# Linear attention, soft mixture and ELU layer on one core: r scaled on its way out of PSUM, the bonus product read from PSUM, the weight conversion spread over two steps

## The chip, the cores and the metric

The kernel runs on one core of one Trainium2 chip. Its time is device microseconds (us) of one execution; the figure for the kernel before is the median of three runs.

## The reference

Three layers follow each other, all in float32. The attention has 4 sequences of 768 tokens and 8 heads of 48 columns; its output, 3072 tokens by 384 columns, goes through a soft mixture of 8 experts with 4 slots each, and then through a dense layer of width 2048.

```python
for t in range(S):                       # attention
    cur = einsum('bhd,bhe->bhde', u * k[t], v[t])
    y[t] = einsum('bhd,bhde->bhe', r[t], state + cur)
    state = w * state + einsum('bhd,bhe->bhde', k[t], v[t])
logits = x @ phi                         # soft mixture: 32 slots
slot_in = softmax(logits, over tokens).T @ x
slot_out[e] = relu(slot_in[e] @ w1[e]) @ w2[e]
z = softmax(logits, over slots) @ slot_out
h = z @ w_in                             # dense layer
out = where(h > 0, h, exp(min(h, 0)) - 1) @ w_out
```

`w_in` and `w_out` come as float64. The chip has no float64 arithmetic here, so the kernel reads each number as two 32-bit words and builds a float32 from them.

## The kernel before, in words

The order on every engine is written out by hand: an engine runs its instructions in the order in which the code issues them, and one that waits holds up all behind it on that engine.

**The attention** cuts the 3072 tokens into 24 chunks of 128 (`NCH`), six to a sequence. The loop `for s in range(-2, NCH)` is a software pipeline over three chunks. In step s it does:

- for chunk s+2: load r and k a step or two ahead, multiply them by tables of powers of w (`scale`, L515: r on GpSimd, k on VectorE, into `rkm`), and turn both by TensorE (`turn`: `ps_r`, `ps_k`), copied out of PSUM by ScalarE to `rT` and `kT`.
- for chunk s+1: add k'v to the state in PSUM (`update`, `pu`), carry the state over (`state`, `t1` on VectorE, `qc` on GpSimd, `qb` on ScalarE), the scores `ps_a` and their mask (`causal`, `am`), the elementwise product of rT and kT (`prod`, `qd`, VectorE) whose sums give the bonus term with u (`bonus_a`, `bonus_b`: `ps_b`, `bt`, `ps_c`, `bs`, and `bv` on GpSimd), and the part of the rows that comes from the earlier state (`before`, into `py`).
- for chunk s: the rest of its rows (`rows_a`, into `py`), their sum with the bonus (`rows_b`, `x`, VectorE), and their turn (`x_T`, `ps_x`).

Three chunks make a group, and a group's logits and slot sums (`part`: `slots_a` to `slots_f`) are dealt out over the following steps by `extra()`, one entry at a time.

**The conversion** of the first 10 of 16 tiles of `w_in` and `w_out` runs in the same loop, one piece of 384 columns a step in steps 0 to 19: `wide_load` brings the raw words into one of two buffers in `scr`, `wide_a` is two ScalarE instructions, `wide_b1`, `b2`, `b3` and `c` are four of VectorE, `wide_d` two of GpSimd. The expert weights (`load_we`) are fetched in the loop as well, on the same queue of SyncE (SP) as r, k, v and the raw words.

**The experts** follow: `up` and `down` of two halves of four experts (a = 0, 1), `turn(a)` between them, `turn_so(a)` behind `down(a)`; ScalarE meanwhile copies all turned weights of the second softmax (`turn_c_b`, `cT`) and splits the converted `w_out` in two (`split`). **The dense layer** is last; the change leaves it alone.

The pools of PSUM that matter are `pt_p`, two buffers that `ps_r`, `ps_x` and `ps_k` take in turn, and `pm_p`, two buffers for the bonus and the slots. `rkm` and `kT` have one buffer, `rT` two.

## Time and profile before

| | |
|---|---|
| median of three runs (lowest to highest) | 472.33 us (471.44 to 473.89) |
| the profiled execution, its own time | 471.74 us |
| its span, first to last instruction | 470.0 us |
| TensorE's clock, mean granted | 0.985 of 2.4 GHz |
| busy: TensorE, VectorE, ScalarE, GpSimd | 89%, 79%, 60%, 40% of the span |
| fetched from memory, written | 51.96 MB, 4.72 MB |

The profiled execution is one program run taken by the hardware profiler; its busy shares are means over three layers that have different limits, so a change to one layer is read in that layer's stretch. In the views, PE is TensorE, PEld its weight loads, DVE VectorE, ACT ScalarE, POOL GpSimd, SP SyncE. L515 is line 515 of the kernel before.

### The profile page before, as it was taken

How to read it: one execution, taken by the hardware profiler on the slowest of the kernel's cores; microseconds unless marked ns; L12 is line 12 of the kernel's file. 1: busy time of each engine (PE TensorE's matmuls, PEld its weight loads, DVE VectorE, ACT ScalarE, POOL GpSimd, SP SyncE). 2: the span in 40 equal slices, each digit the busy share in tenths (PEclk: the TensorE clock that was granted, in tenths of full speed). 3: DMA queues.
4: the chain of work that ended last, by engine and by line, in shares of the span. 5: the costliest groups of instructions: out<-in, count | busy, mean ns of one | idle time of the engine just before them, and what ended most of it. 6: DMA issues, size and time to landing. Idle time of an engine off the chain costs nothing.

```text
span 470.0 us, 10112 instructions
## 1 busy us (share of the span) xinstructions
PE 416.3 (89%) x4013; PEld 365.3 (78%) x4013; DVE 373.7 (79%) x550; ACT 281.4 (60%) x512; POOL 188.9 (40%) x186
## 2 busy tenths in 40 slices
PE   6788788797888898995999899989999999999995
PEld 6677677676776685343899789979998989999994
DVE  5489999979989854533787999996999987787851
ACT  3355455454564452293778787865879677776740
POOL 2276776666866731400000235431224314224440
PEclk9799999989999999999899999999999999999999
DMA  8848899998999987670000111121111001011112
GB/s 124 183 94 232 189 262 257 271 280 206 244 262 273 231 275 237 234 270 1 0 2 0 33 35 34 35 67 35 34 35 33 1 0 51 35 52 67 69 69 73
DMA packets 97575, 57.41 MB, mean 122 GB/s; under 512 B 77808, under 2 KB 89328, under 8 KB 97520
## 3 DMA queue, kind: packets, MB, share of 16 engines
q1 hardware_dynamic: 96704, 56.64, 44.0%
q8 instruction: 33, 0.54, 0.5%
q14 instruction: 22, 0.18, 0.1%
q10 hardware_dynamic: 816, 0.05, 0.1%
HBM read 51.96 MB, written 4.72 MB: 121 GB/s over the span
## 4 chain that ended last, share of the span: by engine, by line
PE 46%; DVE 9%; ACT 5%; issue 4%; POOL 0%; ACTq 0%; DVEq 0%
PE fo L1258 11%; PE fo L1261 11%; PE fo L1259 11%; PE fh L1213 3%; DVE ex L1227 3%; DVE ex L1232 3%; PE pd L1035 2%; PE ph L1013 2%; ACT th L1221 2%; ACT acc L1195 1%; PE phm L1131 1%; ACT gh L1240 1%; ACT ex L1224 1%; PE py L613 1%; DVE acc L1202 0%
## 5 line engine op out<-in xcount | busy, mean ns | idle before, releaser
L1258 PE MATMUL fo<-wh,gh 128*128 128x384 f32 x384 | 131.8, 343 | 7.0 <-ACT gh L1240 3.7
L1259 PE MATMUL fo<-wl,gh 128*128 128x384 f32 x384 | 130.3, 339 | 0.0
L1261 PE MATMUL fo<-wh,gl 128*128 128x384 f32 x384 | 121.9, 339 | 0.2 <-DVE gl L1243 0.2
L1258 PEld LDWEIGHTS fo<-wh,gh 128*128 128x128 f32 x384 | 72.5, 189 | 13.9 <-ACT acc L1195 6.5
L1227 DVE SCALAR_TENSOR_TENSOR ex<-ex,th 128x1024 f32<-128x1024 f32 (+1 forms) x52 | 62.1, 1194 | 23.3 <-ACT ex L1224 23.0
L336 POOL TENSOR_TENSOR cv<-raw,cv 128x384 f32<-128x384 f32 x12 | 19.8, 1652 | 138.2 <-DVE cv L333 65.9
L1221 ACT ACTIVATE th<-fh 128x1024 f32<-128x1024 f32 (+1 forms) x53 | 50.3, 949 | 41.1 <-PE fh L1213 41.1
L1243 DVE TENSOR_TENSOR gl<-ex,gh 128x1024 fp32r<-128x1024 f32 (+1 forms) x52 | 72.0, 1385 | 2.6 <-ACT gh L1240 2.2
L1259 PEld LDWEIGHTS fo<-wl,gh 128*128 128x128 f32 x384 | 72.6, 189 | 1.8
L1261 PEld LDWEIGHTS fo<-wh,gl 128*128 128x128 f32 x384 | 71.9, 189 | 0.5 <-DVE gl L1243 0.5
L1232 DVE SCALAR_TENSOR_TENSOR ex<-ex,fh 128x1024 f32<-128x1024 f32 (+1 forms) x52 | 58.7, 1130 | 0.1
L1224 ACT ACTIVATE ex<-fh 128x1024 f32<-128x1024 f32 (+1 forms) x53 | 50.3, 950 | 9.5 <-DVE gl L1243 9.4
L1240 ACT CAST gh<-ex 128x1024 fp32r<-128x1024 f32 (+1 forms) x52 | 51.5, 991 | 5.9 <-DVE ex L1232 4.7
L1200 POOL TENSOR_TENSOR acc<-os,acc 128x384 f32<-128x384 f32 x20 | 29.0, 1486 | 49.6 <-ACT os L1199 49.6
L602 POOL TENSOR_TENSOR bv<-vd,bs 128x384 f32<-128x384 f32 x24 | 28.3, 1180 | 13.6 <-ACT bs L597 11.5
L1213 PE MATMUL fh<-cT,mst 128*128 128x512 f32 x96 | 30.6, 400 | 2.8 <-DVE ex L1232 2.8
L560 DVE TENSOR_TENSOR am<-ps_a,mask 128x512 f32<-128x512 f32 x48 | 30.6, 675 | 1.5 <-PE ps_a L555 1.5
L529 ACT COPY rT<-ps_r 128x512 f32<-128x512 f32 x24 | 14.1, 587 | 28.5 <-PE ps_r L522 28.5
L533 DVE TENSOR_TENSOR qd<-rT,kT 128x512 f32<-128x512 f32 x24 | 28.9, 1202 | 2.0 <-ACT kT L526 2.0
L522 PE MATMUL ps_r<-ident,rkm 128*128 128x128 f32 x96 | 15.7, 286 | 16.6 <-POOL rkm L515 15.8
L522 PEld LDWEIGHTS ps_r<-ident,rkm 128*128 128x128 f32 x96 | 10.1, 140 | 25.2 <-POOL rkm L515 22.9
L555 PE MATMUL ps_a<-rT,kT 64*128 64x128 f32 x384 | 28.8, 291 | 0.2 <-ACT kT L526 0.2
(170 smaller groups left out, 737.4 us busy)
## 6 DMA issues: line engine op xcount, KB each, us to landing
we<-in_moe_w_dram SPq DMA_DIRECT2D x14, 768.0 KB, 7.8
we<-in_moe_w_dram SPq DMA_DIRECT2D x16, 512.0 KB, 5.8
rk<-in_r_dram SPq DMA_DIRECT2D x24, 192.0 KB, 5.4
rk<-in_k_dram SPq DMA_DIRECT2D x24, 192.0 KB, 4.8
vd<-in_v_dram SPq DMA_DIRECT2D x24, 192.0 KB, 5.3
out_dram<-acc SPq DMA_DIRECT2D x24, 192.0 KB, 1.9
we<-in_moe_w_dram SPq DMA_DIRECT2D x16, 256.0 KB, 5.2
scr<-in_moe_w_out_dram SPq DMA_DIRECT2D x10, 384.0 KB, 4.2
```

The lines of the kernel that those rows point to most:

```text
L560: nc.vector.tensor_tensor(out=am[n, a], in0=aps[a], in1=mask.unsqueeze(1).to_broadcast([128, HP, 128]), op=ALU.mult)
L1200: nc.gpsimd.tensor_tensor(out=a, in0=os_, in1=a, op=ALU.add)
L1213: nc.tensor.matmul(out=ph[n][:, i, :], lhsT=mst[(f + i) // 8][:, 128 * ((f + i) % 8):128 * ((f + i) % 8) + 128], rhs=cT[:, TB * blk:TB * b ...
L1221: nc.scalar.activation(out=th[n][:, s], in_=ph[n][:, s], func=ACTF.Tanh, scale=0.5)
L1224: nc.scalar.activation(out=ex[n][:, s], in_=ph[n][:, s], func=ACTF.Exp)
L1227: nc.vector.scalar_tensor_tensor(out=ex[n][:, s], in0=ex[n][:, s], scalar=1.0, in1=th[n][:, s], op0=ALU.add, op1=ALU.mult)
L1232: nc.vector.scalar_tensor_tensor(out=ex[n][:, s], in0=ex[n][:, s], scalar=0.0, in1=ph[n][:, s], op0=ALU.min, op1=ALU.max)
L1240: nc.scalar.copy(out=gh[n][:, s], in_=ex[n][:, s])
L1243: nc.vector.tensor_tensor(out=gl[n][:, s], in0=ex[n][:, s], in1=gh[n][:, s].bitcast(F32), op=ALU.subtract)
L1258: nc.tensor.matmul(out=o, lhsT=gh[n][:, i, s], rhs=wh, start=(f == first), stop=False)
L1259: nc.tensor.matmul(out=o, lhsT=gh[n][:, i, s], rhs=wl, start=False, stop=False)
L1261: nc.tensor.matmul(out=o, lhsT=gl[n][:, i, s], rhs=wh, start=False, stop=(f == final))
```

## The change

Five edits, all in the attention loop, its end, and the order of the experts.

1. r is no longer scaled before it is turned. It is loaded into `rp` (two buffers with zeroed gaps), turned raw, and VectorE multiplies it by the table `vt` as it leaves PSUM for `rT`. GpSimd's `scale` of r and ScalarE's copy of `ps_r` are gone; the table is no longer turned.
2. The bonus product `qd` reads k from PSUM (`ps_k`), right behind `kT`'s copy, and is issued in `turn(1, n)` at the end of the step before; `prod` is gone.
3. `wide_b1` moves from VectorE to GpSimd, `wide_a` from the end of a step to the start of the next, `wide_b3` and `wide_c` to the end of the step, and `wide_d` to the next step. The raw words have three buffers.
4. In the last step the three entries of the group before come first, with the logits of two of the last three chunks, so that only the third chunk's logits follow its turn.
5. Among the experts `turn(1)` comes before `down(0)`, `turn_so(0)` behind `down(1)`, and one split moves behind `down(0)`.

```diff
@@ -315,4 +315,4 @@
 
-    def wide_b1(raw, a):
-        nc.vector.tensor_scalar(
+    def wide_b1(raw, a, eng=None):
+        (eng or nc.vector).tensor_scalar(
             out=a.bitcast(F32), in0=a.bitcast(F32), scalar1=EXP_LO, scalar2=EXP_HI, op0=ALU.max, op1=ALU.min
@@ -411,5 +411,5 @@
         pw = at2.tile([128, 2, HP, 65], F32, tag="am", name="pw", bufs=3)
-        vt = at2.tile([128, HP, 128], F32, tag="am", name="vt", bufs=3)
+        vt = ae1.tile([128, HP, 128], F32, name="vt")
         vk = at2.tile([128, HP, 128], F32, tag="am", name="vk", bufs=3)
-        wrk = ae1.tile([128, 2, H, D], F32, name="wrk")
+        wk = ae1.tile([128, H, D], F32, name="wk")
         ri = at1.tile([128, HP, 17], F32, name="ri")
@@ -459,7 +459,6 @@
             nc.scalar.copy(out=vk[:, :, 64:128], in_=pw[:, 1, :, 1:65])
-            for i, t in ((0, vt), (1, vk)):
-                ps = pt_p.tile([128, 512], F32, tag="pt", name="ps_wk")
-                for p in range(HP):
-                    nc.tensor.transpose(out=ps[:, 128 * p:128 * p + 128], in_=t[:, p, 0:128], identity=ident)
-                nc.scalar.copy(out=wrk[:, i], in_=ps.rearrange("p (h d) -> p h d", d=64)[:, :, 0:D])
+            ps = pt_p.tile([128, 512], F32, tag="pt", name="ps_wk")
+            for p in range(HP):
+                nc.tensor.transpose(out=ps[:, 128 * p:128 * p + 128], in_=vk[:, p, 0:128], identity=ident)
+            nc.scalar.copy(out=wk, in_=ps.rearrange("p (h d) -> p h d", d=64)[:, :, 0:D])
 
@@ -492,3 +491,4 @@
 
-        rkm = ae1.tile([128, 2, H, 64], F32, name="rkm")
+        rp = [ae2.tile([128, H, 64], F32, name=f"rp{i}", bufs=1) for i in range(2)]
+        km = ae1.tile([128, H, 64], F32, name="km")
         kT = ae1.tile([128, HP, 128], F32, name="kT")
@@ -500,9 +500,11 @@
 
-        def load_rk(n, which=(0, 1)):
+
+        def load_r(n):
             b, c = divmod(n, NC)
-            s = slice(C * c, C * c + C)
-            for i in which:
-                a = (r, k)[i]
-                rk[i, n] = ae2.tile([128, H, D], F32, tag=f"rk{i}", name=f"rk{i}", bufs=2)
-                nc.sync.dma_start(out=rk[i, n], in_=a[b, :, s, :].rearrange("h p d -> p h d"))
+            nc.sync.dma_start(out=rp[n % 2][:, :, 0:D], in_=r[b, :, C * c:C * c + C, :].rearrange("h p d -> p h d"))
+
+        def load_k(n):
+            b, c = divmod(n, NC)
+            rk[n] = ae2.tile([128, H, D], F32, tag="rk1", name="rk1", bufs=2)
+            nc.sync.dma_start(out=rk[n], in_=k[b, :, C * c:C * c + C, :].rearrange("h p d -> p h d"))
 
@@ -513,6 +515,4 @@
 
-        def scale(i, n, eng=None):
-            (eng or (nc.gpsimd, nc.vector)[i]).tensor_tensor(
-                out=rkm[:, i, :, 0:D], in0=rk.pop((i, n)), in1=wrk[:, i], op=ALU.mult
-            )
+        def scale(n):
+            nc.vector.tensor_tensor(out=km[:, :, 0:D], in0=rk.pop(n), in1=wk, op=ALU.mult)
 
@@ -522,3 +522,4 @@
                 nc.tensor.transpose(
-                    out=ps[:, p, :], in_=rkm[:, i, 2 * p:2 * p + 2, :].rearrange("p a d -> p (a d)"), identity=ident
+                    out=ps[:, p, :], in_=(km if i else rp[n % 2])[:, 2 * p:2 * p + 2, :].rearrange("p a d -> p (a d)"),
+                    identity=ident,
                 )
@@ -526,9 +527,7 @@
                 nc.scalar.copy(out=kT, in_=ps)
+                qd[n] = at2.tile([128, HP, 128], F32, tag="qd", name="qd", bufs=1)
+                nc.vector.tensor_tensor(out=qd[n], in0=rT[n], in1=ps, op=ALU.mult)
             else:
                 rT[n] = at2.tile([128, HP, 128], F32, tag="rT", name="rT", bufs=2)
-                nc.scalar.copy(out=rT[n], in_=ps)
-
-        def prod(n):
-            qd[n] = at2.tile([128, HP, 128], F32, tag="qd", name="qd", bufs=1)
-            nc.vector.tensor_tensor(out=qd[n], in0=rT[n], in1=kT, op=ALU.mult)
+                nc.vector.tensor_tensor(out=rT[n], in0=ps, in1=vt, op=ALU.mult)
 
@@ -542,3 +541,3 @@
                     nc.tensor.matmul(
-                        out=pu[64 * a:64 * a + D, p, :], lhsT=rkm[:, 1, 2 * p + a, 0:D], rhs=vd[n][:, 2 * p + a, :],
+                        out=pu[64 * a:64 * a + D, p, :], lhsT=km[:, 2 * p + a, 0:D], rhs=vd[n][:, 2 * p + a, :],
                         start=True, stop=True,
@@ -785,3 +784,2 @@
         scr = we_p.tile([128, KD * FE], F32, tag="we", name="scr").bitcast(I32)
-        sca = ae1.tile([128, PW], I32, name="sca")
         wiv, wov = win.rearrange("p k f -> p (k f)"), wo.rearrange("p i f -> p (i f)")
@@ -801,4 +799,4 @@
             n = min(PW, NW - PW * j)
-            raw = scr[:, 2 * PW * (j % 2):2 * PW * (j % 2) + 2 * n].rearrange("p (n t) -> p n t", t=2)
-            return raw, (sca[:, :n] if j % 2 else scr[:, 4 * PW:4 * PW + n])
+            raw = scr[:, 2 * PW * (j % 3):2 * PW * (j % 3) + 2 * n].rearrange("p (n t) -> p n t", t=2)
+            return raw, scr[:, PW * (6 + j % 2):PW * (6 + j % 2) + n]
 
@@ -817,2 +815,5 @@
                 raw, a = piece(j)
+                if f is wide_b1:
+                    f(raw, a, nc.gpsimd)
+                    return
                 if f is not wide_d:
@@ -829,6 +830,8 @@
 
-        load_rk(0)
+        load_r(0)
+        load_k(0)
         load_v(0)
         nc.scalar.dma_start(out=phi_sb, in_=phi.rearrange("(k p) c -> p k c", p=128))
-        nc.gpsimd.memset(rkm[:, :, :, D:], 0.0)
+        for t in (*rp, km):
+            nc.gpsimd.memset(t[:, :, D:], 0.0)
         nc.gpsimd.memset(uw, 0.0)
@@ -841,5 +844,5 @@
         tables()
-        load_rk(1)
+        load_r(1)
+        load_k(1)
         load_v(1)
-        scale(0, 0, nc.vector)
         nwe = 0
@@ -854,3 +857,2 @@
         for s in range(-2, NCH):
-            j = s
             now, nxt, ahead = s >= 0, 0 <= s + 1 < NCH, s + 2 < NCH
@@ -859,10 +861,11 @@
                 update(s + 1)
-            if ahead and s > -2:
-                scale(0, s + 2)
-            if j == -1:
-                wide(0, wide_a)
-            if not last:
+            wide(s, wide_a)
+            wide(s, wide_b1)
+            if last:
+                extra()
+                extra()
+                extra()
+                logits(GS - 1, 0, G - 1)
+            else:
                 extra()
-            if ahead:
-                scale(1, s + 2)
             if s > 0 and s % G == 0:
@@ -873,13 +876,11 @@
                 state(s + 1)
-                prod(s + 1)
+            if ahead:
+                scale(s + 2)
             if 2 <= s + 4 < NCH:
-                load_rk(s + 4, (1,))
+                load_k(s + 4)
             if 2 <= s + 3 < NCH:
                 load_v(s + 3)
-            if 2 <= s + 4 < NCH:
-                load_rk(s + 4, (0,))
-            if s < 0:
+            if s < 1:
                 wide_load(s + 2)
             if now:
-                wide(j, wide_b1)
                 for p in range(HP):
@@ -887,2 +888,6 @@
                 rows_b(s)
+                wide(s, wide_b2)
+                wide(s - 1, wide_d)
+                if s >= 1 and s + 2 < NP:
+                    wide_load(s + 2)
             if nxt:
@@ -893,10 +898,3 @@
                 bonus_c(s + 1)
-            if now:
-                wide(j, wide_b2)
-                wide(j, wide_b3)
-                wide(j, wide_c)
-                wide(j, wide_d)
-            extra()
-            if last:
-                extra()
+            if not last:
                 extra()
@@ -904,2 +902,4 @@
                 turn(0, s + 2)
+            if 2 <= s + 4 < NCH:
+                load_r(s + 4)
             if nxt:
@@ -910,5 +910,7 @@
             if last:
-                logits(GS - 1)
+                logits(GS - 1, G - 1, G)
             if nxt:
                 bonus_b(s + 1)
+            wide(s, wide_b3)
+            wide(s, wide_c)
             if ahead:
@@ -917,6 +919,2 @@
                 state_b(s + 1)
-            if j >= 0:
-                wide(j + 1, wide_a)
-                if j + 2 < NP:
-                    wide_load(j + 2)
             if s == NCH - 2:
@@ -927,3 +925,3 @@
                 nwe += 1
-            if j == NP - 1:
+            if s == NP:
                 assert nwe == NWE - 1
@@ -1091,14 +1089,14 @@
     turn_c_b(0)
+    turn(1)
     turn_c_a(1)
     turn_c_a(2)
-    for i in range(0, 4):
+    for i in range(0, 3):
         split(i)
     down(0)
-    turn(1)
     turn_c_b(1)
-    turn_so(0)
     turn_c_b(2)
-    for i in range(4, FA // 2):
+    for i in range(3, FA // 2):
         split(i)
     down(1)
+    turn_so(0)
     turn_so(1)
```

**TensorE, one step in the middle of the loop** (the second half of step s, from the turn of r on; the names in brackets are the engines or queues whose signal the instruction waits for). Before:

```order
L522 MATMUL ps_r<-ident,rkm 128x128 [waits Pool_49]
L522 MATMUL ps_r<-ident,rkm 128x128 x3
L613 MATMUL py<-qb_145,rT 128x96 [waits DVE_49,Activation_49]
L613 MATMUL py<-qb_145,rT 128x96 x3
L645 MATMUL ps_x<-ident,x 128x128 x3
L595 MATMUL ps_c<-ident,bt 128x128 [waits Activation_49]
L522 MATMUL ps_k<-ident,rkm 128x128 [waits Activation_49]
```

And now:

```order
L522 MATMUL ps_r<-ident,rp_144 128x128 [waits DMAHW3_49]
L522 MATMUL ps_r<-ident,rp_144 128x128 x3
L612 MATMUL py<-qb_147,rT 128x96 [waits DVE_49,Activation_49]
L612 MATMUL py<-qb_147,rT 128x96 x3
L644 MATMUL ps_x<-ident,x 128x128 x3
L594 MATMUL ps_c<-ident,bt 128x128 [waits Activation_49]
L522 MATMUL ps_k<-ident,km 128x128 [waits DVE_49]
```

The order is the same. The turn of r waits for its transfer where it waited for GpSimd, and the turn of k waits for VectorE (which must have emptied r's buffer) where it waited for ScalarE.

**VectorE, one step in the middle of the loop**, from the carry of the state to the next one; `scr` is the raw words under conversion, `al` and `nmx` the maxima of a group's logits. Before:

```order
L583 TENSOR_TENSOR t_147<-qc,pu 128x192 [waits Pool_49]
L533 TENSOR_TENSOR qd<-rT,kT 128x512 [waits Activation_49]
L317 TENSOR_SCALAR scr<-scr 128x384 [waits Activation_49]
L636 TENSOR_TENSOR x<-py,bv 128x384 [waits PE_49,Pool_49]
L560 TENSOR_TENSOR am<-ps_a,mask 128x512 [waits PE_49] x2
L322 TENSOR_SCALAR scr<-scr 128x384 [waits DVE_49]
L328 SCALAR_TENSOR_TENSOR scr<-scr 128x384 [waits DMAHW3_49,DMAHW2_49,DVE_49]
L333 TENSOR_SCALAR scr<-scr 128x384 [waits DVE_49]
L670 TENSOR_REDUCE al<-ps_l 96x1 [waits PE_49]
L671 TENSOR_SCALAR nmx<-al,nmx 96x1 [waits DVE_49]
L515 TENSOR_TENSOR rkm<-rk_856,wrk 128x8x48 [waits DMAHW0_49,PE_49]
```

And now:

```order
L582 TENSOR_TENSOR t_149<-qc,pu 128x192 [waits PE_49,Pool_49]
L517 TENSOR_TENSOR km<-rk_726,wk 128x8x48 [waits DMAHW7_49]
L635 TENSOR_TENSOR x<-py,bv 128x384 [waits PE_49,Pool_49]
L322 TENSOR_SCALAR scr<-scr 128x384 [waits Pool_49]
L559 TENSOR_TENSOR am<-ps_a,mask 128x512 [waits PE_49] x2
L532 TENSOR_TENSOR rT<-ps_r,vt 128x512 [waits PE_49]
L328 SCALAR_TENSOR_TENSOR scr<-scr 128x384 [waits DMAHW1_49,DMAHW2_49,DVE_49,Activation_49]
L333 TENSOR_SCALAR scr<-scr 128x384 [waits DVE_49]
L529 TENSOR_TENSOR qd<-rT,ps_k 128x512 [waits Activation_49]
L669 TENSOR_REDUCE al<-ps_l 96x1
L670 TENSOR_SCALAR nmx<-al,nmx 96x1 [waits DVE_49]
```

Still nine instructions of attention and conversion: the first of the conversion (L317) is gone, the scaling of r (L532) has come in, L322 stands before the masks and waits for GpSimd, and `qd` has moved to the end, where it waits for ScalarE.

**ScalarE at the start of the loop**, from the first `kT` to the second. Before:

```order
L526 COPY kT<-ps_k 128x512 [waits PE_49]
L313 ACTIVATE scr<-scr 128x384 [waits DMAHW5_49]
L314 ACTIVATE scr<-scr 128x384
L573 COPY bt<-ps_b 128x128 [waits PE_49]
L529 COPY rT<-ps_r 128x512 [waits PE_49]
L597 COPY bs<-ps_c 128x8 [waits PE_49]
L526 COPY kT<-ps_k 128x512 [waits DVE_49,PE_49]
```

And now:

```order
L527 COPY kT<-ps_k 128x512 [waits PE_49]
L572 COPY bt<-ps_b 128x128 [waits PE_49]
L596 COPY bs<-ps_c 128x8 [waits PE_49]
L527 COPY kT<-ps_k 128x512 [waits PE_49,Activation_49]
L589 COPY qb_148<-qc 64x4x48 [waits Pool_49]
L589 COPY qb_148<-qc 64x4x48
L313 ACTIVATE scr<-scr 128x384 [waits DMAHW4_49]
```

The first piece's conversion, which waits for a transfer, stood ahead of `bt`; now it stands behind the second `kT` and `qb`.

## Rows read from the trace of the kernel before

**Rows 1.** Busy time by stretch: us of each engine, clock, DMA share, GB/s.

```profile
core 0: us, PE busy (x) PEld busy (x) DVE busy (x) ACT busy (x) POOL busy (x), PEclk, DMA share, GB/s
45.00:173.00 128.00, 106.61 (x1843) 91.50 (x1841) 112.97 (x204) 66.99 (x186) 88.33 (x86) 0.99 0.97 257
166.00:173.00 7.00, 6.70 (x142) 6.09 (x138) 4.91 (x9) 3.43 (x10) 3.47 (x4) 1.00 1.10 359
```

**Rows 2.** Timeline of VectorE, the scaling of k in steps 0 and 21.

```profile
18.28 0.77 DVE L515 TENSOR_TENSOR rkm<-rk,wrk 128x384 f32<-128x384 f32 x1 [4.87 <-PE pu L542]
...
166.04 0.82 DVE L515 TENSOR_TENSOR rkm<-rk,wrk 128x384 f32<-128x384 f32 x1 [1.52 <-PE pu L542]
```

**Rows 3.** Timeline of VectorE, step 18: start, us, instruction, [idle before, releaser].

```profile
145.71 0.54 DVE L515 TENSOR_TENSOR rkm<-rk,wrk 128x384 f32<-128x384 f32 x1
146.18 0.34 DVE L583 TENSOR_TENSOR t<-qc,pu 128x192 f32<-128x192 f32 x1
146.44 1.24 DVE L533 TENSOR_TENSOR qd<-rT,kT 128x512 f32<-128x512 f32 x1
147.60 0.98 DVE L317 TENSOR_SCALAR scr<-scr 128x384 f32<-128x384 f32 x1
148.51 0.55 DVE L636 TENSOR_TENSOR x<-py,bv 128x384 f32<-128x384 f32 x1
148.97 1.27 DVE L560 TENSOR_TENSOR am<-ps_a,mask 128x512 f32<-128x512 f32 x2
150.17 0.34 DVE L322 TENSOR_SCALAR scr<-scr 128x384 int32<-128x384 int32 x1
150.55 0.56 DVE L328 SCALAR_TENSOR_TENSOR scr<-scr 128x384 int32<-128x384 int32 x1
151.14 0.36 DVE L333 TENSOR_SCALAR scr<-scr 128x384 int32<-128x384 int32 x1
151.41 0.28 DVE L670 TENSOR_REDUCE al<-ps_l 96x1 f32<-96x128 f32 x1
151.73 0.21 DVE L671 TENSOR_SCALAR nmx<-al,nmx 96x1 f32<-96x1 f32 x1
152.44 0.63 DVE L515 TENSOR_TENSOR rkm<-rk,wrk 128x384 f32<-128x384 f32 x1 [0.50 <-PE pu L542]
```

**Rows 4.** Timeline of TensorE, the same step, from the turn of r.

```profile
149.50 0.66 PE L522 MATMUL ps_r<-ident,rkm 128*128 128x128 f32 x4 [0.60 <-POOL rkm L515]
...
151.30 0.60 PE L522 MATMUL ps_k<-ident,rkm 128*128 128x128 f32 x4
...
154.64 0.43 PE L568 MATMUL ps_b<-qd,uw 128*32 128x128 f32 x8 [0.23 <-DVE qd L533]
```

**Rows 5.** Timeline of GpSimd, the same step.

```profile
145.85 1.28 POOL L337 TENSOR_TENSOR wo<-scr,sca 128x384 f32<-128x384 f32 x1
147.09 1.28 POOL L602 TENSOR_TENSOR bv<-vd,bs 128x384 f32<-128x384 f32 x1
148.33 1.11 POOL L515 TENSOR_TENSOR rkm<-rk,wrk 128x384 f32<-128x384 f32 x1
149.40 0.51 POOL L584 TENSOR_TENSOR qc<-t,w 128x192 f32<-128x192 f32 x1
```

**Rows 6.** Instructions that touch qd and the masks: ns least/median/most, first and last start.

```profile
L533 DVE TENSOR_TENSOR qd<-rT,kT x24: 678/1242/1507, 11.5 to 172.4; 128x512 f32<-128x512 f32 x24
...
L560 DVE TENSOR_TENSOR am<-ps_a,mask x48: 672/674/692, 12.1 to 174.9; 128x512 f32<-128x512 f32 x48
```

**Rows 7.** Timeline of ScalarE, step 18.

```profile
151.93 0.59 ACT L526 COPY kT<-ps_k 128x512 f32<-128x512 f32 x1
```

**Rows 8.** Timeline at the start of the loop, ScalarE and TensorE.

```profile
14.91 0.54 ACT L313 ACTIVATE scr<-scr 128x384 f32<-128x384 f32 x1 [4.03 <-DMA scr<-in_moe_w_in_dram]
...
16.09 0.48 PE L595 MATMUL ps_c<-ident,bt 128*128 128x128 f32 x1 [2.76 <-ACT bt L573]
```

**Rows 9.** Timeline of TensorE in the last step.

```profile
178.99 0.85 PE L708 MATMUL ps_s<-x,et 128*32 128x384 f32 x6 [0.98 <-DVE et L701]
```

**Rows 10.** Timeline of ScalarE, behind the second half of the experts.

```profile
212.34 0.58 ACT L1039 ACTIVATE so<-pd,rz 128x384 f32<-128x384 f32 x1 [0.38 <-PE pd L1035]
```

## The prediction

> **What bounds the kernel now.** I read the shares of each engine first and set them aside, since they are means over three layers; then busy time by stretch, then one step of the attention loop on each engine. From step 0 to step 21 VectorE's scaling of k starts at 18.28 and at 166.04 us [rows 2], so 21 steps take 147.76 us, 7.04 us each. In the same loop VectorE is busy 112.97 of 128 us, TensorE 106.61, GpSimd 88.33, ScalarE 66.99, and the DMA engines show a share of 0.97 [rows 1]. No engine is the bound by itself; two are close to it, and the transfers are close too.
>
> One step shows how they hold each other up. VectorE's nine instructions of step 18 follow each other without a gap from 145.71 to 151.41, 5.70 us; the two of the slots take it to 151.94, and then it waits 0.50 for TensorE's update of the state before the next step begins at 152.44 [rows 3]. TensorE goes from the turn of r at 149.50 to the end of `ps_b` at 155.07 (154.64 + 0.43) with one wait of 0.23, so its work in a step is 5.34 us; ahead of the turn of r it waited 0.60 for GpSimd [rows 4]. GpSimd came late because its product for r starts at 148.33, behind the last conversion product and `bv`, at 145.85 and 147.09 [rows 5], and the conversion products cannot start before VectorE's last conversion instruction of that piece. So there is a ring: VectorE's conversion, GpSimd's products and r, TensorE's turn of r and all behind it, the update of the state, VectorE's scaling of k, the conversion again. The reader should see in these rows that r on GpSimd is the one link that is in the ring only because of where it stands in GpSimd's order.
>
> **The change, part by part.**
>
> *r.* GpSimd loses the 1.11 us product [rows 5] and TensorE's wait for it. VectorE gains a product of 128x512 out of PSUM. The mask product has that shape and source: two start 1.20 us apart from the next instruction, 0.60 each [rows 3], and its duration over 48 runs stays within 672 and 692 ns [rows 6]. I take +0.60. ScalarE loses its copy of `ps_r`, which it had time for: no price. r's transfer is now waited for by TensorE; its buffer is refilled right behind the turn, two steps ahead of the next use, so some 13 us of cover stand over it.
>
> *The bonus product.* In step 18 it takes 1.16 us from start to start, 147.60 - 146.44 [rows 3]; over the run it lies between 678 and 1507 ns with a median of 1242 [rows 6]. The two ends are the same instruction with and without something in its way, and the masks beside it show no such spread. With k out of PSUM it has the masks' form, so 0.60: a gain of 0.56 a step. Against that it stands behind `kT`'s copy and has VectorE's next step queued behind it.
>
> *The conversion.* VectorE loses `wide_b1`, 148.51 - 147.60 = 0.91 us [rows 3]. GpSimd gains it: no row has it there, and the nearest are `qc`, two inputs of 192 columns in 0.51, and `bv`, two of 384 in 1.28 [rows 5]; I take 1.0, between them, which is about what r's product gives back. GpSimd no longer waits for the same step's VectorE, since its products lag by a step. The third buffer gives a piece's transfer more than a step of cover.
>
> *VectorE's sum.* 5.70 - 0.91 - 0.56 + 0.60 = 4.83 us, and 0.53 for the slots as in step 18 [rows 3]: 5.36. TensorE's stays 5.34 and up to 0.85 for a slot product [rows 9], about 5.9 with a mean share of those.
>
> *The new wait.* TensorE can turn k only when VectorE has emptied r's buffer. From there it is 0.60 for the turn [rows 4] and 0.59 for `kT`'s copy [rows 7] until the bonus product may start, with two handovers some 1.25. VectorE fills 0.9 of it with the last two conversion instructions (150.55 to 151.41) [rows 3]. About 0.35 is left, with the next step's carry, k, rows and masks queued behind it: 5.7 us. The Trainium skill, "PSUM — Partial Sum Buffer", section "PSUM bank collisions raise a hardware error", says that two engines must not read one PSUM bank at the same time. That speaks against reading `ps_k` twice: it is why the product has to stand behind the copy, and without the rule these 0.35 us would not be there. No run here shows the rule; the order of VectorE shows the wait.
>
> *What the two neighbours do to each other.* VectorE keeps four instructions that read only the ordinary memory: k's scaling and three of the conversion. What such an instruction can lose to a GpSimd product is the 0.56 of the bonus product, 1242 - 678 ns [rows 6]. The bounds a step are none of the four, which leaves TensorE's 5.9, and all four, 5.7 + 4 x 0.56 = 7.9. GpSimd is free for over a microsecond of a step but it now has work at the moments at which the conversion runs, since its products no longer wait for it; I take one and a half of the four, 0.84, and so **6.5 us** a step. The Trainium skill, "SBUF — State Buffer", section "Who interferes with whom", has the rule for it: the two engines share a port pair that one holds for a whole instruction, and VectorE needs it for two inputs from that memory, not for one from PSUM. The rows of the masks and of the bonus product agree. By the rule alone the sum stays between the same bounds, since it says who may wait and not how often.
>
> *The start.* ScalarE waits 4.03 us for the first raw words with `bt` queued behind, and TensorE waits 2.76 for `bt` [rows 8]. In the new order `bt` is ahead: -2.7. What is late next is r's buffer on VectorE, behind the masks, which is the step's usual pace.
>
> *The last step and the experts.* The slot product of 0.85 moves from behind the last rows to ahead of them, and its 0.98 us wait becomes a wait for the rows' sum [rows 9]; TensorE has the same work before the last logits, so I take 0 (0.5 either way). Among the experts ScalarE, not TensorE, is full: ahead of its last output it is idle 0.38 us [rows 10], and no order of the same copies can give more: -0.4.
>
> *The sum.* 21 x (7.04 - 6.5) = 11.3, and 2.7 and 0.4: 14.4 off a span of 470.0 is 455.6. The profiled execution took 471.74 by its own time, 1.74 more than its span, so **457 us**; the median of the runs is 0.6 above the profiled one, which I leave inside the range.
>
> **The rivals.**
>
> *TensorE or the transfers become the bound.* If the neighbours do not meet, the step falls to TensorE's 5.9 or to what the transfers allow. The share of 0.97 in the loop looks like a ceiling, but a stretch of 7 us reached 1.10 [rows 1]; the same packets would then fit in 7.04 x 0.97 / 1.10 = 6.2 us. At 6.2 the gain is 17.6 + 3.1, and the time 451. For it: the long cover of every load. Against it: VectorE has no slack left by then.
>
> *Half of the gain is lost between VectorE and GpSimd.* Two of the four instead of one and a half and the step is 6.8: 5.0 + 3.1 off, 464. For it: GpSimd's `bv` and last product fall where the last two conversion instructions stand, and those are now ahead of the bonus product, on the path. The same time comes out if 0.97 is the transfers' true ceiling, 7.04 x 0.97 = 6.8.
>
> *Slower.* One mechanism can turn the sign: VectorE's order. `qd` now closes the step, and all of the next step stands behind it. If three of the four stand behind a GpSimd product the step is 5.7 + 3 x 0.56 = 7.4, 7.6 more over 21 steps, less the 3.1 of the start and the experts: 476. It decides from 7.04 + 3.1 / 21 = 7.19 us a step, that is from 1.5 us of such waits. Against it: the two instructions that met a GpSimd product oftenest, the bonus product and `wide_b1`, have left that list.
>
> *No change.* The step ends at 7.0 to 7.1 and only the start is kept: 469 to 471.
>
> **How the numbers follow.** The forecast has 0.47, the lower step 0.18, the half gain 0.21, slower 0.08, no change 0.06. The predicted time is that of the first. The range runs from 448, a step of 6.05, to 468, a step of 7.0; it leaves out the slower case, most of no change and the very end below. Half a per cent, 2.4 us, is about what a measurement of this kernel can tell from no change. Faster by more has 0.86, within it 0.06, slower 0.08.
>
> **What the profile after should show.** The scaling of k should start some 6.5 us apart. TensorE's turn of r should wait for nothing, GpSimd least of all. The bonus product should last 0.68 us in every step and be preceded by a short wait for ScalarE. TensorE's 2.76 us wait at the start should be gone. If I am wrong it will be seen in VectorE's three conversion instructions and k's scaling: durations far over their shortest, beside GpSimd's products; or in TensorE waiting at the turn of r for a transfer, which would be the loads. ScalarE's last expert output should start 0.4 us or less sooner, counted from `up`.

## The result, and the profile after

The changed kernel takes 466.38 us, median of 4 runs (464.58 to 467.28), where the kernel before took 471.92 on the same chip (471.44 to 473.89): a ratio of 0.987, 95% interval 0.9828 to 0.9912. That is faster by 1.3%, and within the range given, but 5.5 us where about 15 were forecast. The profiled execution took 467.28 by its own time, with a span of 465.5 against 470.0.

First the pace of the loop, VectorE's scaling of k in steps 0 and 21, which answers to [rows 2] (line numbers are those of the changed kernel):

```profile
16.28 0.55 DVE L517 TENSOR_TENSOR km<-rk,wk 128x384 f32<-128x384 f32 x1
...
162.25 0.55 DVE L517 TENSOR_TENSOR km<-rk,wk 128x384 f32<-128x384 f32 x1
```

(162.25 - 16.28) / 21 = 6.95 us a step, against 7.04 before and 6.5 forecast. From step 0 to the first `up` it is 165.13 us, before 168.08 (18.28 to 186.36). So the 4.5 us of span are: 2.0 at the start, 2.95 in the loop, 0.36 among the experts, less 0.8 that the dense layer took longer in this profile. The gain of 0.09 a step is small beside what the clock does: TensorE's granted clock was 0.83 between 88 and 98 us before (one step of 9.15 us, 88.55 to 97.70) and 0.88 between 52 and 60 us after, so for part of each stretch the lower of its two levels, 1.2 GHz.

One slow step on VectorE, which answers to [rows 3]:

```profile
128.14 0.54 DVE L517 TENSOR_TENSOR km<-rk,wk 128x384 f32<-128x384 f32 x1
128.61 0.55 DVE L635 TENSOR_TENSOR x<-py,bv 128x384 f32<-128x384 f32 x1
130.47 1.17 DVE L322 TENSOR_SCALAR scr<-scr 128x384 int32<-128x384 int32 x1 [1.32 <-POOL scr L317]
131.56 1.28 DVE L559 TENSOR_TENSOR am<-ps_a,mask 128x512 f32<-128x512 f32 x2
132.75 0.68 DVE L532 TENSOR_TENSOR rT<-ps_r,vt 128x512 f32<-128x512 f32 x1
133.35 0.54 DVE L328 SCALAR_TENSOR_TENSOR scr<-scr 128x384 int32<-128x384 int32 x1
133.93 0.36 DVE L333 TENSOR_SCALAR scr<-scr 128x384 int32<-128x384 int32 x1
134.85 0.69 DVE L529 TENSOR_TENSOR qd<-rT,ps_k 128x512 f32<-128x512 f32 x1 [0.56 <-ACT kT L527]
```

VectorE stands still for 1.32 us ahead of `wide_b2` (L322), with the masks and r's scaling queued behind it; the instruction then takes 1.17, where its shortest was 0.34 [rows 3]. What it waits for, on GpSimd (answers to [rows 5]), ScalarE and TensorE:

```profile
128.95 1.49 POOL L317 TENSOR_SCALAR scr<-scr 128x384 f32<-128x384 f32 x1 [2.01 <-ACT scr L313]
130.40 1.02 POOL L336 TENSOR_TENSOR scr<-scr 128x384 f32<-128x384 f32 x1
```

```profile
126.47 0.59 ACT L527 COPY kT<-ps_k 128x512 f32<-128x512 f32 x1 [0.90 <-PE ps_k L522]
126.95 0.71 ACT L589 COPY qb<-qc 64x192 f32<-64x192 f32 x2
...
128.29 0.57 ACT L313 ACTIVATE scr<-scr 128x384 f32<-128x384 f32 x1
```

```profile
133.48 0.66 PE L522 MATMUL ps_k<-ident,km 128*128 128x128 f32 x4 [2.34 <-DVE rT L532]
```

Read as a chain this is a new ring: the turn of k, its copy to `kT`, `qb`, `wide_a` (L313) on ScalarE; `wide_b1` (L317), 1.49 us on GpSimd; `wide_b2`, the masks and r's scaling on VectorE; the next turn of k, for which TensorE waits 2.34 us. The waits and lengths over the whole loop (16 to 165 us; the columns after the count are busy us, mean ns, idle before and its releasers):

```profile
L322 DVE TENSOR_SCALAR scr<-scr 128x384 int32<-128x384 int32 x20 | 15.5, 776 | 11.8 <-POOL scr L317 11.0
L529 DVE TENSOR_TENSOR qd<-rT,ps_k 128x512 f32<-128x512 f32 x22 | 15.1, 687 | 4.6 <-ACT kT L527 4.6
L333 DVE TENSOR_SCALAR scr<-scr 128x384 int32<-128x384 int32 x20 | 14.5, 726 | 0.7
L517 DVE TENSOR_TENSOR km<-rk,wk 128x384 f32<-128x384 f32 x22 | 13.3, 603 | 0.0
L328 DVE SCALAR_TENSOR_TENSOR scr<-scr 128x384 int32<-128x384 int32 x20 | 12.7, 637 | 0.0
```

The wait for GpSimd stands in 10 of the 20 steps that convert; over 21 steps it is 0.52 a step, that for `kT` 0.22. Over their shortest (0.34, 0.36, 0.54, 0.54) the four instructions that read ordinary memory lose 0.44, 0.37, 0.06 and 0.10, together 0.97. Of that, 0.81 falls on `wide_b2` and `wide_c`, which have one input each. In the changed kernel `wide_b2` never has its length of before, in ns least/median/most before and after:

```profile
L322 DVE TENSOR_SCALAR scr<-scr x10: 342/343/352, 23.2 to 150.2; 128x384 int32<-128x384 int32 x10
```

```profile
L322 DVE TENSOR_SCALAR scr<-scr x20: 654/655/1175, 18.2 to 150.8; 128x384 int32<-128x384 int32 x20
```

(before, the other ten pieces go through `sca`, with the same length.)

The bonus product and the start, which answer to [rows 6] and [rows 8]:

```profile
L529 DVE TENSOR_TENSOR qd<-rT,ps_k x24: 675/688/690, 11.1 to 166.6; 128x512 f32<-128x512 f32 x24
```

```profile
13.61 0.27 ACT L572 COPY bt<-ps_b 128x128 f32<-128x128 f32 x1 [2.51 <-PE ps_b L567]
```

```profile
13.97 0.29 PE L594 MATMUL ps_c<-ident,bt 128*128 128x128 f32 x1
```

The product lasts 0.68 to 0.69 in every step; `bt` waits for TensorE's own work and no longer for raw words, and TensorE not at all for `bt`.

### The profile page after: what moved, and what is told of

Its sections match the earlier page's. It is cut to its first block, busy times and chain, and to the rows that moved or that the text cites. A ratio compares the mean times of both kernels' runs of the same rounds, so it can differ in the third digit from the quotient of the medians.

```text
span 465.5 us, 9991 instructions
## 1 busy us (share of the span) xinstructions
PE 416.9 (90%) x4009; PEld 365.4 (78%) x4009; DVE 369.6 (79%) x553; ACT 268.5 (58%) x487; POOL 186.3 (40%) x185
## 4 chain that ended last, share of the span: by engine, by line
PE 50%; DVE 16%; POOL 13%; ACT 10%; issue 8%; DMA 3%; POOLq 0%; DVEq 0%; ACTq 0%; SPq 0%
PE fo L1256 12%; PE fo L1257 11%; PE fo L1259 11%; POOL scr L317 5%; PE fh L1211 3%; DVE ex L1230 3%; DVE ex L1225 3%; DMA scr<-in_moe_w_out_dram 2%; POOL scr L336 2%; PE ph L1011 2%; POOL bv L601 2%; DVE am L559 2%; ACT scr L313 1%; PE ps_a L554 1%; ACT th L1219 1%
## 5 line engine op out<-in xcount | busy, mean ns | idle before, releaser
L317 POOL TENSOR_SCALAR scr<-scr 128x384 f32<-128x384 f32 x20 | 30.8, 1538 | 35.7 <-ACT scr L313 35.7
L522 PE MATMUL ps_k<-ident,km 128*128 128x128 f32 x96 | 15.9, 290 | 23.5 <-DVE rT L532 22.2
L646 ACT COPY xT<-ps_x 128x384 f32<-128x384 f32 x24 | 11.5, 479 | 38.6 <-PE ps_x L644 38.6
L522 PEld LDWEIGHTS ps_k<-ident,km 128*128 128x128 f32 x96 | 10.4, 143 | 28.4 <-DVE rT L532 26.7
L527 ACT COPY kT<-ps_k 128x512 f32<-128x512 f32 x24 | 14.1, 587 | 30.4 <-PE ps_k L522 30.2
```

The costliest lines, as they stand in the source:

```text
L317: (eng or nc.vector).tensor_scalar(out=a.bitcast(F32), in0=a.bitcast(F32), scalar1=EXP_LO, scalar2=EXP_HI, op0=ALU.max, op1=ALU.min)
```

## The experiments

Each time stands beside runs of the kernel before on the same chip, and the ratio is to those. The step is measured as above, and the stretch is from step 0's scaling of k to the first `up`; both are from one profile each, the time is a median.

| kernel | median us | ratio (95%) | step | stretch |
|---|---|---|---|---|
| before | 471.92 | | 7.04 | 168.1 |
| changed | 466.38 | 0.987 (0.983 to 0.991) | 6.95 | 165.1 |
| e1 `wide_b2` late | 461.37 | 0.975 (0.971 to 0.979) | 6.78 | 162.2 |
| e2 no `wide_b1` | 460.03 | 0.975 (0.971 to 0.978) | 6.60 | 159.1 |
| e3 `wide_b1` on VectorE | 472.13 | 1.000 (0.998 to 1.002) | 7.26 | 171.7 |
| e4 fewer loads of r | 467.74 | 0.992 (0.988 to 0.996) | 6.89 | 163.9 |
| e5 e2 and e4 | 453.02 | 0.963 (0.959 to 0.966) | 6.26 | 150.6 |
| e6 `wide_a`, `b1` a step early | 461.62 | 0.981 (0.976 to 0.985) | 6.74 | 160.7 |
| e7 product from `kT` | 466.62 | 0.992 (0.989 to 0.995) | 6.99 | 165.8 |
| e8 before, start moved | 468.36 | 0.994 (0.991 to 0.997) | 7.11 | 169.7 |
| e9 before, r alone | 467.83 | 0.992 (0.990 to 0.995) | 6.96 | 166.2 |
| e10 tails of before | 466.38 | 0.988 (0.982 to 0.994) | 7.03 | 165.8 |
| e11 `wide_b1` of two inputs | 466.68 | 0.990 (0.986 to 0.993) | 6.98 | 165.7 |
| e12 `wide_b1` with one bound | 462.76 | 0.982 (0.977 to 0.986) | 6.83 | 162.6 |
| e13 e6, four raw buffers | 458.18 | 0.968 (0.963 to 0.973) | 6.54 | 156.6 |
| e14 e6 and e1 | 460.77 | 0.978 (0.972 to 0.984) | 6.58 | 157.3 |
| e15 e13 and e1 | 455.49 | 0.968 (0.964 to 0.972) | 6.44 | 154.5 |

A difference of 0.1 in the step says nothing by itself. Up to step 21 the loop of e10 is the changed kernel's, and its step is 7.03 where that has 6.95: its granted clock was 0.81 from 133 to 141 us and 0.86 from 154 to 163, where the changed kernel had 1.00 in both.

**The wait for GpSimd (e1 to e4).** The theory is the ring above; the rival, that the transfers hold the step.

```diff
@@ e1 @@
-                wide(s, wide_b2)
...
+            wide(s, wide_b2)
             wide(s, wide_b3)
@@ e2 @@
-                    f(raw, a, nc.gpsimd)
+                    pass
@@ e3 @@
-            wide(s, wide_b1)
...
+                wide(s, wide_b1)
                 wide(s, wide_b2)
...
-                    f(raw, a, nc.gpsimd)
+                    f(raw, a, nc.vector)
@@ e4 @@
-            if 2 <= s + 4 < NCH:
+            if 2 <= s + 4 < 4:
                 load_r(s + 4)
```

> The changed kernel (466.4 us) with one line moved: wide_b2 of VectorE goes from ahead of the masks to behind the turn's product rT, beside wide_b3. In the changed kernel VectorE waited 11.0 us in 10 steps ahead of the masks for GpSimd's wide_b1. Theory of the ring (that wait is what the steps lose over the 6.5 us forecast): the wait goes, steps come to 6.4 to 6.5, some 10 us off, 456 us. Theory of the neighbours (VectorE and GpSimd only lengthen each other's instructions, 0.9 us a step): the same four instructions still meet GpSimd, no change, 465 to 468. Theory of the transfers (DMA share 0.99 is the ceiling): no change, 465 to 468, and waits for transfers in place of the wait for wide_b1.

> The changed kernel without wide_b1, the clamp of the conversion's exponents, which is left out altogether; order otherwise as it was. The ring: GpSimd's 1.5 us are gone from between ScalarE and VectorE's wide_b2, so the wait ahead of the masks goes: 455 us. The neighbours: GpSimd is 1.5 us lighter a step and wide_b2, b3 and c come back towards their shortest, 0.9 us a step at most: 450 to 460 as well, but seen in their durations. The transfers: no change, 465 to 468.

> The changed kernel with wide_b1 back on VectorE, directly ahead of wide_b2, so that it waits for ScalarE alone. The ring: the wait for GpSimd goes, 0.5 us a step, and VectorE gets 0.3 to 1.0 us a step: 460 to 468, near no change. The neighbours: GpSimd's products come earlier and away from the conversion's last instructions, the durations of b3 and c fall: 455 to 460. The transfers: no change.

> The changed kernel without the loads of r from chunk 4 on (20 of 24 loads are left out; the later chunks are computed from the r of chunks 2 and 3). A third of the small packets is gone, some 0.9 us of transfer a step. The transfers: steps fall by up to 0.9 us, 450 us or less. The ring and the neighbours: no change, 464 to 467.

With `wide_b2` late, and again with `wide_b1` gone, the wait of 11.0 us is gone and 5 to 6 us of time with it, so the ring was real. It is about half of what was expected of it (455 to 456): in e1 TensorE now waits 6.4 us for v's transfer and VectorE 2.9 each for TensorE's `ps_a` and `ps_r`, in e2 TensorE waits 11.4 us for v's transfer and VectorE 8.0 for `kT`. Shorter instructions are not the reason in e2: `wide_b2` lasts 0.82 there, longer than the 0.78 of the changed kernel, and only `wide_c` is shorter (0.58 for 0.73).

Without 20 of the 24 loads of r, on the other hand, the time stays where it was: the transfers do not hold the changed kernel. The two profiles agree step for step. The changed kernel starts step 5 1.32 us after e4 (52.30 and 50.98), step 6 2.58 after it and step 21 2.57 after it, and the one step in which they part is that of the lower clock; ahead of it, from 30 to 52 us, TensorE was busy 17.06 us in both (the changed kernel, then e4; the columns are the stretch, its length, busy us of TensorE, weight loads, VectorE, ScalarE and GpSimd, clock, transfers' share, GB/s):

```profile
52.00:60.00 8.00, 7.65 (x132) 6.36 (x128) 7.10 (x15) 3.33 (x10) 4.93 (x6) 0.88 0.96 263
```

```profile
52.00:60.00 8.00, 7.45 (x129) 6.04 (x124) 7.83 (x15) 3.28 (x9) 6.54 (x7) 1.00 0.82 236
```

With `wide_b1` back on VectorE (e3) nothing is left of the change's gain, which is worse than all three readings expected. There `wide_b1` lasts 0.78, `wide_b2` 0.92, and VectorE waits 9.8 us for `kT` (15 to 168 us). The granted clock was 0.94 from 15 to 165 us, where the changed kernel had 0.99, so a part of the loss may be the clock's; how much is not shown.

**The transfers behind it (e5).** The diffs of e2 and e4 together.

> The changed kernel without wide_b1 and with r loaded for the first four chunks alone (the other chunks are computed from these r). Without wide_b1 alone the step was 6.60 us and TensorE's update of the state waited 11.4 us for v's transfer in 6 steps. If the transfers are what holds the step at 6.6: the waits for vd go, the step falls to 6.3 or less, and the time to 454 or less. Rival: the engines hold it at 6.6 and the waits for transfers only take slack: 459 to 461.

The step falls from 6.60 to 6.26, and TensorE's 11.4 us of waits for v's transfer are gone: with the wait for GpSimd gone, the transfers are next.

**The place or the length of `wide_b1` (e6, e11, e12).**

```diff
@@ e6 @@
-            wide(s, wide_a)
-            wide(s, wide_b1)
+            if s == 0:
+                wide(0, wide_a)
+                wide(0, wide_b1)
...
                 bonus_c(s + 1)
+            if now:
+                wide(s + 1, wide_a)
+                wide(s + 1, wide_b1)
@@ e11 @@
-                    f(raw, a, nc.gpsimd)
+                    nc.gpsimd.tensor_tensor(
+                        out=a.bitcast(F32), in0=a.bitcast(F32), in1=ones[:, :a.shape[1]], op=ALU.mult
+                    )
@@ e12 @@
-                    f(raw, a, nc.gpsimd)
+                    nc.gpsimd.tensor_scalar(
+                        out=a.bitcast(F32), in0=a.bitcast(F32), scalar1=EXP_LO, scalar2=None, op0=ALU.max
+                    )
```

> The changed kernel with wide_a and wide_b1 of the next piece issued a step earlier, behind bonus_c, with a third buffer for their output; VectorE's order is that of the changed kernel. Theory (ring through kT's copy, wide_a, GpSimd's wide_b1 and VectorE's wide_b2): VectorE's wait for wide_b1 goes, the step falls from 6.95 to 6.6 to 6.8 us, 459 to 463. Rival (the time goes to the length of the products on GpSimd and to neighbours on the shared memory, not to the wait): GpSimd has the same work, so 465 to 468, with the wait moved elsewhere.

> The changed kernel with wide_b1 as a product of two inputs on GpSimd (by a tile of ones), which leaves out the bounds on both sides. If the form with one input and two bounds is what takes 1.5 us, this takes 1.0 to 1.15, as the other products of this size do, VectorE's 11.0 us of waits for it fall to 5 or less, and the time to 462 to 464. Rival (the place sets it, beside VectorE's instructions): it takes 1.4 to 1.6 as well, and the time stays at 466 to 467.

> The changed kernel with one of the two bounds of wide_b1, the upper one, left out; it stays a one-input instruction of GpSimd. If the two operations make its length, it takes 0.9 to 1.1 us and the time falls to 462 to 464; if the form with one input does, 1.4 to 1.5 us and 466 to 467.

`wide_b1` by tile, in ns least/median/most, in the changed kernel, with two inputs, and with one bound:

```profile
L317 POOL TENSOR_SCALAR scr<-scr x20: 1487/1505/1750, 16.7 to 149.3; 128x384 f32<-128x384 f32 x20
```

```profile
L819 POOL TENSOR_TENSOR scr<-scr,ones x20: 999/1007/1221, 15.4 to 149.1; 128x384 f32<-128x384 f32 x20
```

```profile
L817 POOL TENSOR_SCALAR scr<-scr x20: 1166/1167/1371, 15.3 to 145.7; 128x384 f32<-128x384 f32 x20
```

With two inputs it takes 1.007, the length that the prediction had priced, and the wait falls to 6.1 us, yet the time stays. VectorE's lines of e11 (16 to 160 us) say where it went:

```profile
L322 DVE TENSOR_SCALAR scr<-scr 128x384 int32<-128x384 int32 x20 | 19.7, 985 | 6.1 <-POOL scr L819 6.1
L517 DVE TENSOR_TENSOR km<-rk,wk 128x384 f32<-128x384 f32 x20 | 16.2, 810 | 0.0
```

`wide_b2` and k's scaling each take 0.21 longer than in the changed kernel and `wide_c` 0.19 less (0.54): 0.23 a step, against the 0.25 of wait that went (4.9 us in 20 pieces). So both readings that I set against each other fall short: length and place act together. With one bound it takes 1.17 us, between the two lengths that I had expected; the wait goes to 7.8 with little lost elsewhere, and the time falls by 2.5 (by the ratios) to 3.6 us (by the medians). Issued a step earlier, at its full length, it is waited for once and no more (e6): 3 to 5 us. There ScalarE, which now asks for the raw words a step earlier, waits 25 us for them, and `kT` is queued behind.

**The other edits (e7 to e10).**

```diff
@@ e7 @@
-                nc.vector.tensor_tensor(out=qd[n], in0=rT[n], in1=ps, op=ALU.mult)
+                nc.vector.tensor_tensor(out=qd[n], in0=rT[n], in1=kT, op=ALU.mult)
@@ e8, on the kernel before @@
-            if j == -1:
-                wide(0, wide_a)
...
-            if j >= 0:
+            if j >= -1:
                 wide(j + 1, wide_a)
@@ e9, on the kernel before @@
-            if ahead and s > -2:
-                scale(0, s + 2)
...
-                nc.scalar.copy(out=rT[n], in_=ps)
+                nc.vector.tensor_tensor(out=rT[n], in0=ps, in1=vt, op=ALU.mult)
```

e10 undoes edits 4 and 5 as a whole: those parts of the change's diff in reverse.

> The changed kernel with the bonus product read from kT in the ordinary memory and no longer from PSUM; its place in the order is the same. As the prediction priced it, the product goes from 0.69 back to some 1.24 us, and the step by up to 0.56: 472 to 478. Rival: at the end of the step, where it now stands, it meets no GpSimd product and has the wait for kT ahead of it in any case: under 1 us slower, 466 to 468.

> The kernel before with one thing moved: the first piece's wide_a goes from the middle of step -1 to its end, behind bt. As the prediction priced the start: 2.7 us faster, 469. Rival: what is late next (the first scaling of k, r's buffer) takes most of it: 0 to 1 us faster, 471 to 472.

> The kernel before with the first edit alone: r is turned raw and VectorE scales it out of PSUM; the bonus product, the conversion, the last step and the experts are those of before. Theory (VectorE sets the step): it gains 0.60 us of its own, TensorE's 0.60 wait for GpSimd goes but was only its slack, and GpSimd's 1.11 less makes room for its conversion products; the step stays at 7.0 to 7.3, 470 to 477. Rival (r on GpSimd was the link that closed the ring): the step falls by the 0.5 to 0.6 that TensorE waited, 459 to 462.

> The changed kernel with the last step and the experts' order of before; the loop up to the last step is that of the changed kernel. From the two traces: the stretch from the scaling of k in step 21 to the first `up`, 19.16 us, goes back to 20.3, and from there to the last output of the experts from 25.62 to 25.98: 1.5 us slower, 468. Rival (the prediction: the last step is worth 0, and the 1.16 us come from the conversion's lag and the loop's last steps): only 0.4 slower, 466 to 467, and the stretch stays at 19.2.

The bonus product of e7, from ordinary memory at the new place, and that of e9, the same instruction at the old place:

```profile
L529 DVE TENSOR_TENSOR qd<-rT,kT x24: 676/692/835, 10.7 to 165.9; 128x512 f32<-128x512 f32 x24
```

```profile
L537 DVE TENSOR_TENSOR qd<-rT,kT x24: 678/1242/1514, 11.3 to 169.4; 128x512 f32<-128x512 f32 x24
```

0.69 and 1.24 us: it is the place that makes it short; the source shows only in the longest of the 24, 0.84 in e7 against 0.69 out of PSUM. At the end of the step GpSimd stands idle, waiting for `wide_a` (2.01 us in the step above). The start by itself gains 2.5 us (e8). r by itself (e9) gains 3.7 by its ratio, and its profile starts step 0 1.1 us sooner. It lies between the two expectations: VectorE's busy time rose by 5.0 us only, from 122.7 to 127.7 of 135 (20 to 155 us), though the new product alone takes 13.0 there. Other instructions got shorter, k's scaling from 0.74 to 0.66 and `wide_b1` from 0.96 to 0.82 in the mean.

The tails, which are the last step and the experts, are worth nothing in the median (e10). My reading that the last step had gained 1.16 us falls: with the old order the stretch from step 21 to the first `up` is 18.26 us, shorter than the 19.16 of the new one. The 0.36 of the experts show in the profile alone (from `up` to the start of the last output 25.97 against 25.62).

**What the floor is (e13 to e15).** e13 adds to e6 a fourth buffer of raw words, e14 adds to e6 the late `wide_b2` of e1, e15 has all three.

```diff
@@ e13, on e6 @@
+        scx = ae1.tile([128, 2 * PW], I32, name="scx")
...
+            raw = scx[:, :2 * n] if j % 4 == 3 else scr[:, 2 * PW * (j % 4):2 * PW * (j % 4) + 2 * n]
...
-                if s >= 1 and s + 2 < NP:
-                    wide_load(s + 2)
+                if s + 3 < NP:
+                    wide_load(s + 3)
```

> The kernel with the next piece's wide_a and wide_b1 issued a step earlier, and a fourth buffer of raw words, so that a piece is fetched three steps ahead and no longer two. There ScalarE waited 25 us for raw words in 13 steps with the copy to kT queued behind, and VectorE 18.8 us for kT. If the fetch was only issued too late: these waits go, the step falls from 6.74 to 6.5, and the time to 457. Rival (the rate of all transfers is the floor): the same bytes arrive no sooner, the waits move to v's transfer, and the time stays at 460 to 462.

> The same earlier wide_a and wide_b1, with three buffers, and wide_b2 beside wide_b3 behind the scaling of r. If VectorE's wait and its slowed instructions are what is left, VectorE has neither a wait for GpSimd nor one ahead of the masks, but three instructions in a row beside GpSimd's bv: 459 to 461. Rival (the transfers' rate): no change against either edit alone, 461 to 462.

> All three at once: the next piece's wide_a and wide_b1 a step earlier, four buffers of raw words fetched three steps ahead, and wide_b2 beside wide_b3. With wide_b2 late VectorE was busy 113.4 of 135 us in the loop where it had been 123.7 with four buffers, but waited 17.8 us for kT behind late raw words. If these waits go as they did with four buffers (to 8), the step falls from 6.54 to 6.3, and the time to 453 to 455. Rival (the rate of all transfers holds the step at 6.5): the waits move to v's transfer, 457 to 459.

With the raw words fetched earlier the waits for them fall from 25 us to 1.3 and the step to 6.54, the step that was forecast. e14 shows no difference from e1 or e6 that these runs can tell. e15 is the fastest in the median of those that leave nothing out, though its interval and e13's overlap. What waits there, from the list of waits:

```profile
PE pu L541 <- DMA vd<-in_v_dram: 9.4, 6, 2.9
DVE qd L529 <- ACT kT L527: 6.2, 9, 1.7
```

TensorE waits for v's transfer: 5.1 us in e13, 9.4 here. So part of what VectorE gave (120.4 of 130 us busy in e13, 113.2 in e15, from 20 to 150 us) is spent on waiting for transfers, and both expectations of e15 hold in part. What holds its step at 6.44 is not shown: TensorE too is busy for 116.85 of these 130 us, at a granted clock of 0.97.

## Why the prediction was right and wrong

**The sum, term by term.** The forecast step was 4.83 of VectorE's instructions, 0.53 of slots, 0.35 of waiting for `kT` and 0.84 between neighbours, which is 6.55, taken as 6.5. Measured are 0.22 for `kT` and 0.97 between neighbours, which nearly cancel. Not in the sum at all is the 0.52 of VectorE's wait for GpSimd. With it the terms give 4.83 + 0.53 + 0.22 + 0.97 + 0.52 = 7.07, against 6.95 measured; 0.53 is the slots' share in one step and too much for the mean. The whole loop says the same without the shares:

```profile
16.00:165.00 149.00, 125.34 (x2127) 106.16 (x2122) 130.74 (x248) 66.45 (x190) 102.82 (x100) 0.99 0.95 240
```

VectorE is busy 130.74 of 149 us, 6.10 a step where the forecast had 6.20, and idle 18.26, 0.85 a step where the forecast had 0.35. So VectorE's work was priced rightly and its waiting was not.

That the 0.84 came so near is in part luck. The prediction let each of the four lose up to 0.56; `wide_b2` lost up to 0.83, and the two with two inputs 0.06 and 0.10 in the mean.

**The step that failed is "The conversion".** It said that GpSimd gains `wide_b1` and took 1.0 us for it, as time of GpSimd, and noted only that GpSimd no longer waits for VectorE. That VectorE now waits for GpSimd stood in the order of the change (L322 with Pool, ahead of the masks), and was not followed back: `wide_b1` starts behind `wide_a`, which stands behind `kT` and `qb` on ScalarE, so it begins too late for `wide_b2`. The price was off as well (1.5 for 1.0), but the price alone is not the cause: at 1.0 with two inputs (e11) the kernel is no faster, at 1.17 with one bound (e12) it gains 2.5 to 3.6 us, and at its full 1.5 but issued a step earlier (e6) 3 to 5. With the wait taken away by an earlier `wide_a` and an earlier load (e13) the step is 6.54 and the time 458.2, against the forecast of 6.5 and 457. Neither of the two signs of being wrong that the prediction named is this wait.

**The bonus product** has the length that was said, 0.69, for a reason that was wrong: out of ordinary memory, at the same place, it is as short in the median (e7). The term came out by luck. The rule of the Trainium skill on shared ports ("SBUF — State Buffer", "Who interferes with whom") says which instructions may meet, not where they do. By it a one-input `tensor_scalar` can also take the shared pair, where its operands allow it, and whichever of the two engines comes first then keeps the other waiting for its whole instruction. The step above agrees: `wide_b2`, of that form, starts at 130.47, behind the start of a GpSimd product that lasts from 130.40 to 131.42, and ends at 131.64.

**r on VectorE** cost the 0.60 a step that was said (132.75 to 133.35 in the step above) and took TensorE's wait for GpSimd away, as said: no turn of r waits for GpSimd. But the ring that the prediction drew through r did not hold the step by itself: r alone (e9) takes it from 7.04 to 6.96, and all five edits together to 6.95. VectorE is busy 6.58 us a step in e9 (127.7 of 135) and 6.10 in the changed kernel, so the bonus product and the conversion did free 0.48 of it; its idle time rose by as much, from 0.38 to 0.85 a step.

**The start** gave 2.0 of the predicted 2.7 in this profile. Between 9 and 16 us its granted clock was 0.76, so for part of it the lower of its two levels, 1.2 GHz; e7, the same order there, had 1.00 and started step 0 at 14.92, 1.4 sooner (columns as above):

```profile
9.00:16.00 7.00, 6.55 (x101) 5.64 (x101) 4.80 (x9) 2.20 (x6) 1.57 (x2) 0.76 0.99 186
```

```profile
9.00:16.00 7.00, 6.40 (x125) 5.44 (x125) 5.99 (x12) 3.22 (x8) 2.27 (x3) 1.00 0.98 190
```

At the full clock, then, the start gives 3.4 in the profile (18.28 to 14.92), more than predicted. By runs, the start alone is worth 2.5 (e8).

**The last step** was put at 0 and the experts at 0.4; e10 agrees with the first, and its profile with the second.

**The rivals.** By its time the kernel lies between "half of the gain is lost" (464) and "no change" (469 to 471). Neither cause given for the first is the one: the neighbours took about what was forecast, and 0.97 is no ceiling of the transfers, whose share is 1.01 in e15 (20 to 150 us). By its step, 6.95, it is nearest to "no change", a step of 7.0 to 7.1 with the start kept, which had 0.06 and no mechanism.

## What to carry to other kernels

When an instruction moves to another engine, price three things: its length there, what it waits for there, and who now waits for it. Follow each new wait in the order back through every engine until it closes or ends; if it closes, the length of the ring is a bound on the step, whatever the sums per engine say. And when an instruction's length varies between two values, look at what runs beside it at each place before putting the difference down to its operands. A step taken from one profile holds the clock of that profile: compare the granted clock stretch by stretch before reading a difference of one or two per cent.

## What the runs showed of the hardware

In the place of `wide_b1`, a GpSimd instruction on 128x384 float32 took 1.505 us in the median with one input and two operations, 1.167 with one input and one operation (e12), and 1.007 with two inputs and one operation (e11): here the form with one input was the longer one. VectorE's shift and mask of the same tile took 0.34 us in the kernel before, with no GpSimd product beside it in the step of [rows 3] and [rows 5], and up to 1.17 beside a GpSimd product in the changed kernel.
